# Re-ordering the start-up of a fused cosine-attention and feed-forward kernel: loads of batch 0, engine assignment, w_out's third quarter, and unit order

## The chip, the cores and the metric

The kernel runs on one core of a Trainium2 chip. The metric is device time in microseconds (us) of the whole program. Engines: PE (TensorE) multiplies matrices into PSUM; DVE (VectorE), ACT (ScalarE) and POOL (GpSimd) work element by element; SP (SyncE) issues nearly all DMAs. Each engine works through its own instructions in program order.

## The reference

Linear attention with cosine weights, then a feed-forward layer (batch 8, 8 heads, 576 positions, head size 64; w_in 512x2048, w_out 2048x512; all float32):

```python
theta = pi/2 * pos / 576
phi(x, c, s) = concat(relu(x)*c, relu(x)*s)        # 64 -> 128 features
q_p, k_p = phi(q, cos, sin), phi(k, cos, sin)
kv  = einsum('bhsf,bhsd->bhfd', k_p, v);  z = k_p.sum(over s)
num = q_p @ kv;  den = q_p @ z + 1e-6
x   = (num / den) -> (4608 tokens, 512)
h   = x @ w_in;  g = max(0.01*h, h);  out = g @ w_out
```

## The kernel before

Each batch has 512 main positions (four tiles j = 0..3 of 128) and 64 tail positions. Batch b's main positions form token group g = b; the tails of all batches are the ninth group. Everything is cast to float16 for PE.

For a group PE does this. `q_transpose` turns q_p of a tile (eight transposes), and an engine copies the result to `qpT`. `kv_half(b, hg)` multiplies k_p with v for heads 0-3 (hg 0) or 4-7 (hg 1), two extra columns of ones giving z; ACT copies the result to `kv`. `num_half(g, jp, hg)` multiplies qpT of two tiles (jp 0 or 1) with kv, and `divide` on DVE (three instructions) writes `xp`. `x_transpose_half` turns xp (four transposes) and ACT copies it to `xT`. The "half" forms serve groups 0 and 1; later groups use `kv_all`, `num`, `x_transpose`.

`ffn1(g, m)` is h for columns of w_in numbered m (16 of them): four products over the chunks c of 128 rows of w_in, 128x512 each, two m's to a PSUM tile, which ACT turns into `g` with one leaky relu. `ffn2(g, 4*tt + part)` is a unit of four products of w_out, with one quarter (`part`) of its rows, for output tile tt of the group; after part 3 `ffn2_out` copies the output tile to SBUF and stores it. `idle(n)` issues n products whose result nobody reads.

Loads go out from SP in program order: in the kernel before, q of batch 0 in two halves of heads, the tails of k and v (four pieces of 64 KB, rows of 256 bytes), k and v by halves of heads (`load_halves`), w_in in eight pieces of 512 KB, then two quarters of w_out, q of batch 1, its k and v tails, the other two quarters, k and v of batch 1 by halves, and so on. Loads share seven `stage` buffers. POOL casts w_in, DVE casts w_out.

The order of work is written out by hand up to the middle of group 1. From there `weave(units, steps)` runs through feed-forward units that have positions, and ahead of each unit emits every step (`at(pos, ...)`) whose position has come: q_p, k_p, kv, num and transposes of the next group. PSUM is three pools: `h` and `o` with two slots each, `n` with one.

Lines the steps touch: L417 is ffn1's product, L440 ffn2's, L260 and L270 the kv products, L374 and L391 the num_half products and the transposes, L220 and L222 phi on ACT and DVE, L291 and L395 ACT's kv and xT copies, L228 and L230 other copies and casts, L425 the leaky relu.

Of the kernel before, what the change touches and what calls it, by code (L numbers as in the profile page):

```python
# [9 lines left out]
dt = mybir.dt  # L10
# [3 lines left out]
P = 128  # L14
# [4 lines left out]
def kernel(  # L19
# [102 lines left out]
    w1 = [  # L122
        [const.tile([P, 2, 512], dt.float16, name=f"w1_{i}_{cp}") for cp in range(2)]
        for i in range(DFF // 512)
    ]
# [4 lines left out]

    w2v = moe_w_out.rearrange("(i p r) d -> i p r d", p=P, r=4)

    def load_w1(i, cp):

        if cp == 0:
            st["w1", i] = stage.tile([P, NKC, 512], dt.float32, name="w1st", tag="stage")
        sl = slice(2 * cp, 2 * cp + 2)
# [162 lines left out]
    def q_prep(g, j, lo=0, hi=H):  # L300
# [4 lines left out]
        phi_half(DVE, qp[:, lo:hi, 0:D], src[:, lo:hi], cos_t[:, c : c + 1])  # L305
        phi_half(DVE, qp[:, lo:hi, D:F], src[:, lo:hi], sin_t[:, c : c + 1])

    def q_transpose_dma(g, j):
        qpT = qptpool.tile([P, H, P], dt.float16, name="qpT")
# [53 lines left out]
            op=ALU.mult,  # L363
        )

    def num_half(g, jp, hg, where):

        if hg == 0:
            st["xp", g, jp] = qppool.tile([P, 2, H, D], dt.float16, name="xp", tag="qp")
        ps = psum(where, [P, 2, 512], dt.float32, "ps_numh")  # L370
        for o in range(2):
            for hh in range(4):
                h = 4 * hg + hh
                nc.tensor.matmul(  # L374
                    ps[:, o, hh * NE : (hh + 1) * NE],
                    lhsT=st["qpT", g, 2 * jp + o][:, h, :],
                    rhs=kv[g][:, h, :],
                )
        divide(ps, st["xp", g, jp][:, :, 4 * hg : 4 * hg + 4, :])

    def x_transpose_half(g, jp, hg, ps=None, out=True):
# [4 lines left out]
        if ps is None:  # L386
            ps = psum("o", [P, 2, 2 * P], dt.float16, "ps_xth")
        for cc in range(2):
            for o in range(2):
                h = 4 * hg + 2 * cc  # L390
                nc.tensor.transpose(  # L391
                    ps[:, cc, o * P : (o + 1) * P], xp[:, o, h : h + 2, :], ident
                )
        if out:
            nc.scalar.copy(  # L395
                st["xT", g][:, 2 * hg : 2 * hg + 2, jp * 2 * P : (jp + 1) * 2 * P], ps
            )

    def x_transpose(g, j, where="o"):
        xs = st["xs", g, j]  # L400
# [7 lines left out]
    def ffn1(g, m, lo=0, hi=MAIN, chunks=range(NKC), where="h"):  # L408

        if ("g", g) not in st:  # L410
            st["g", g] = gpool.tile([P, NFT, MAIN], dt.float16, name="g")
        if m % 2 == 0 and chunks[0] == 0 and lo == 0:
            st["h", m // 2] = psum(where, [P, 2, MAIN], dt.float32, "ps_h")
        xT = st["xT", g]
        ps = st["h", m // 2]
        for c in chunks:
            nc.tensor.matmul(  # L417
                ps[:, m % 2, lo:hi],
                lhsT=w1[m // 4][c // 2][:, c % 2, m % 4 : 512 : 4],
                rhs=xT[:, c, lo:hi],  # L420
                start=(c == 0 and lo == 0),
                stop=(c == NKC - 1 and hi == MAIN),
            )
        if m % 2 == 1 and chunks[-1] == NKC - 1 and hi == MAIN:
            nc.scalar.activation(st["g", g][:, m - 1 : m + 1, :], ps, AF.Lrelu)  # L425
# [59 lines left out]
    def cast_w1(i, cp, eng):  # L485
        sl = slice(2 * cp, 2 * cp + 2)
        copy(eng, w1[i][cp], st["w1", i][:, sl])

    def cast_w2(i, eng):
        copy(eng, w2[:, 4 * i : 4 * i + 4, :], st["w2", i])  # L490

    for hg in range(2):
        for j in range(2):
            q_prep(0, j, 4 * hg, 4 * hg + 4)
    for j in range(J):
        if j > 1:
            q_prep(0, j)
        q_transpose(0, j, ACT)  # L500
        idle(1)
    kp_tiles(0)
    k_tail(0, DVE, DVE)
    v_tail(0, DVE)
    for j in range(J):
        k_main(0, j, DVE, DVE, 0, 4)
    v_main(0, 0, 4, ACT)
    for j in range(2):
        k_main(0, j, ACT, DVE, 4, 8)
    idle(6)  # L510
    kv_half(0, 0, "o")
    for j in range(2, J):
        k_main(0, j, DVE, DVE, 4, 8)
    v_main(0, 4, 6, DVE)
    v_main(0, 6, 8, ACT)
    idle(1)
    num_half(0, 0, 0, "n")
    num_half(0, 1, 0, "h")
    idle(3)
    kv_half(0, 1, "o")  # L520
    for i in range(NB):
        for cp in range(2):
            cast_w1(i, cp, POOL)
    x_transpose_half(0, 0, 0)
    num_half(0, 0, 1, "n")
    half = 2 * P
    for m in range(2):
        ffn1(0, m, 0, half, range(0, 2))
    x_transpose_half(0, 1, 0)
    for m in range(2, 4):  # L530
        ffn1(0, m, 0, half, range(0, 2))
    num_half(0, 1, 1, "n")
    x_transpose_half(0, 0, 1)
# [37 lines left out]
    def at(pos, f, *args):  # L571
        steps.append((pos, lambda: f(*args)))
# [15 lines left out]
    cast_w2(3, DVE)  # L588
    ps = psum("n", [P, 2, DM], dt.float32, "ps_o")
    for tt in range(2):  # L590
        st["ps_o", 0, 2 + tt] = ps[:, tt]
    steps = []
    for j in range(J):
        at(5 + j, q_transpose, 1, j, ACT, "h")
        at(9, k_main, 1, j, ACT, DVE, 0, 4)
    at(9, v_main, 1, 0, 2, DVE)
    at(9, v_main, 1, 2, 4, ACT)
    order = [(0, 0), (1, 0), (2, 0), (3, 0), (0, 1), (1, 1), (2, 1), (3, 1), (2, 2), (3, 2)]
    weave([(n, f2(0, 4 * tt + part)) for n, (tt, part) in enumerate(order)], steps)
    for tt in (2, 3):  # L600
# [14 lines left out]
    ffn2(0, 3, None)  # L615
    kv_half(1, 1, "h")
    ffn2_out(0, 0, ACT)
    ffn2_mm(0, 1, 12, 14)
    num_half(1, 0, 1, "h")
    num_half(1, 1, 1, "h")  # L620
    ps = psum("n", [P, 2, MAIN], dt.float16, "ps_x")
    for jp in range(2):
        x_transpose_half(1, jp, 0, ps[:, :, jp * 2 * P : (jp + 1) * 2 * P], False)
    nc.scalar.copy(st["xT", 1][:, 0:2, :], ps)  # L624
    ffn2_mm(0, 1, 14, 16)
    ffn2_out(0, 1, DVE)
    ps = psum("o", [P, 2, 2, 2 * P], dt.float16, "ps_x1")
    x_transpose_half(1, 0, 1, ps[:, 0])
    for m in range(2):
        ffn1(1, m, 0, MAIN, range(0, 2))  # L630
    x_transpose_half(1, 1, 1, ps[:, 1])
    for m in range(2, 4):
        ffn1(1, m, 0, MAIN, range(0, 2))
    for m in range(4):
        ffn1(1, m, 0, MAIN, range(2, 4))

    units = []
    for m in range(4, NFT):  # L640
        units.append((8 + m / 2, f1(1, m, "n" if m < 6 else "h")))
    for g in range(1, NG):
        ahead = {1: 8, 2: 4}.get(g, 0)
        order = [f2(g, i) for i in range(ahead)]
# [33 lines left out]
            at(start + j * step + lag, q_transpose_dma, b, j)  # L678

    q_steps(2, 8, 0.4, 0.3)  # L680
    kv_steps(2, 9.7, 0.5, 13, DVE, 2)
    for j in range(J):
        at(13.5 + 1.1 * j, num, 2, j)
        at(14.8 + 1.1 * j, x_transpose, 2, j, "o" if j < 2 else "h")

    load_steps(3, 11, 13, 10)
    q_steps(3, 18, 0.8, 0.8)
# [50 lines left out]
```

## Time and profile before

| | |
|---|---|
| median of 3 runs | 295.70 us (295.67 to 295.79) |
| the profiled execution | 296.48 us, its span 294.7 us |
| granted TensorE clock | 1.00 |
| PE busy | 286.4 us, 97% |
| DVE, ACT, POOL busy | 129.9, 117.9, 11.0 us |
| DMA | 56.93 MB, 193 GB/s on average |

The span runs from the first to the last instruction; what lies around it (1.8 us here) is in the time as well. In a timeline row the first number is the start from the span's beginning, the second the duration of one instruction (or from the first to the last end of several), then engine, line, operation, output and inputs, and in brackets the idle time before it and what ended it. Products on PE overlap: one of 128x512 is followed by the next 0.216 us later, though each is shown longer.

### The profile page before, as it was taken

The numbers are of one execution on the slowest core, as the hardware profiler recorded it, in microseconds if no ns is written. First come the engines' busy times: TensorE is split into PE (matmuls) and PEld (weight loads), VectorE is DVE, ScalarE is ACT, GpSimd is POOL, SyncE is SP. The second block draws the span as 40 slices with busy tenths as digits, with TensorE's granted clock in tenths as the row PEclk, the third lists the DMA queues.
The fourth block names the chain that finished last, engine by engine and source line by source line (L and its number), as shares of the span: only waits on it lengthen the run. The fifth ranks groups of instructions, "written<-read, shape, count | busy, mean of one in ns | idle before, by whom it ended". The sixth has DMA issues, their size and how long they took to land.

```text
span 294.7 us, 4802 instructions
## 1 busy us (share of the span) xinstructions
PE 286.4 (97%) x1932; PEld 153.9 (52%) x1932; DVE 129.9 (44%) x329; ACT 117.9 (40%) x143; POOL 11.0 (4%) x20
## 2 busy tenths in 40 slices
PE   7799999999999999999999999999999999999995
PEld 3585556565465455555545554555445544444444
DVE  6951488945846816823562356233323211000011
ACT  4846366754352722642263226322222232222200
POOL 2064000000000000000000000000000000000000
PEclk9999999999999999999999999999999999999999
DMA  7999999999999999989683997416671211011132
GB/s 222 361 385 406 325 362 331 300 155 336 232 271 325 179 265 335 178 158 332 171 152 82 292 276 148 107 55 145 145 160 51 73 53 38 36 46 60 39 71 71
DMA packets 88773, 56.93 MB, mean 193 GB/s; under 512 B 56880, under 2 KB 81712, under 8 KB 88240
## 3 DMA queue, kind: packets, MB, share of 16 engines
q1 hardware_dynamic: 88672, 56.57, 74.2%
q8 instruction: 15, 0.25, 0.4%
q14 instruction: 6, 0.05, 0.1%
q10 hardware_dynamic: 80, 0.07, 0.1%
HBM read 36.70 MB, written 9.44 MB: 157 GB/s over the span
## 4 chain that ended last, share of the span: by engine, by line
PE 81%; DMA 8%; SPq 6%; ACT 1%; issue 1%; DVE 1%; ACTq 0%
PE ps_h L417 38%; PE ps_o L440 37%; SPq L96 4%; DMA w2st<-in_moe_w_out_dram 4%; DMA w1st<-in_moe_w_in_dram 4%; PE ps_num L339 3%; PE ps_kv L270 2%; SPq L86 1%; DMA out_dram<-osb 1%; SPq L138 1%; ACT vmain L228 1%; SPq L142 1%; PE ps_kv L260 1%; DVE w L230 0%; PE ps_numh L374 0%
## 5 line engine op out<-in xcount | busy, mean ns | idle before, releaser
L417 PE MATMUL ps_h<-xT,w 128*128 128x512 f16 (+1 forms) x592 | 142.6, 373 | 0.3 <-ACT xT L624 0.2
L440 PE MATMUL ps_o<-w,g 128*128 128x512 f16 x560 | 139.5, 379 | 0.3 <-DVE w L230 0.3
L425 ACT ACTIVATE g<-ps_h 128x1024 f16<-128x1024 f32 x72 | 73.5, 1024 | 132.9 <-PE ps_h L417 132.7
L417 PEld LDWEIGHTS <-w 128*128 128x128 f16 x592 | 64.4, 113 | 52.3 <-issue 0.3
L440 PEld LDWEIGHTS <-g 128*128 128x128 f16 x560 | 54.1, 98 | 62.0 <-issue 0.6
L230 DVE COPY osb<-ps_o 128x512 f32<-128x512 f32 x34 | 23.4, 690 | 80.1 <-PE ps_o L440 80.1
L350 DVE TENSOR_SCALAR den<-ps_num 128x8 f32<-128x8 f32 x28 | 4.6, 166 | 52.9 <-PE ps_num L339 52.9
L355 DVE TENSOR_TENSOR xs<-ps_num,rden 128x512 f16<-128x512 f32 x28 | 19.4, 691 | 1.0
L222 DVE TENSOR_SCALAR qp<-qst,cos_t 128x512 f16<-128x512 f32 (+1 forms) x34 | 15.8, 465 | 4.9 <-DMA qst<-in_q_dram 4.9
L222 DVE TENSOR_SCALAR kpm<-kst,sin_t 128x512 f16<-128x512 f32 (+1 forms) x40 | 16.5, 428 | 0.8 <-DMA kst<-in_k_dram 0.8
L222 DVE TENSOR_SCALAR qp<-qst,sin_t 128x512 f16<-128x512 f32 (+1 forms) x34 | 15.8, 465 | 0.0
L339 PEld LDWEIGHTS <-qpT 128*128 128x128 f16 (+1 forms) x256 | 11.2, 101 | 7.3 <-issue 1.7
L222 DVE TENSOR_SCALAR kpm<-kst,cos_t 128x512 f16<-128x512 f32 (+1 forms) x29 | 13.0, 449 | 0.1
L228 ACT CAST vmain<-vst 128x1024 f16<-128x1024 f32 (+1 forms) x14 | 12.9, 953 | 0.4 <-DMA vst<-in_v_dram 0.3
L339 PE MATMUL ps_num<-kv,qpT 128*128 128x66 f16 (+1 forms) x256 | 12.4, 194 | 0.0
L270 PEld LDWEIGHTS <-kpm 128*128 128x128 f16 x256 | 10.5, 97 | 2.6 <-DVE kpm L222 0.7
L228 ACT COPY qpT<-ps_qt 128x1024 f16<-128x1024 f16 x8 | 7.8, 1019 | 7.0 <-PE ps_qt L329 7.0
L162 PE MATMUL ps_idle<-blank 128*128 128x512 f16 x28 | 9.1, 462 | 1.2 <-DVE blank L157 1.2
L230 DVE CAST w<-w2st 128x2048 f16<-128x2048 f32 x4 | 4.9, 1228 | 10.7 <-DMA w2st<-in_moe_w_out_dram 10.7
L230 POOL CAST w<-w1st 128x1024 f16<-128x1024 f32 x8 | 8.3, 1042 | 15.1 <-DMA w1st<-in_moe_w_in_dram 15.0
L270 PE MATMUL ps_kv<-vmain,kpm 128*128 128x66 f16 x192 | 8.1, 193 | 0.0
L354 DVE RECIPROCAL rden<-den 128x8 f32<-128x8 f32 x36 | 7.3, 203 | 1.2
(57 smaller groups left out, 97.1 us busy)
## 6 DMA issues: line engine op xcount, KB each, us to landing
out_dram<-osb SPq DMA_DIRECT2D x32, 256.0 KB, 2.5
qst<-in_q_dram SPq DMA_DIRECT2D x7, 1024.0 KB, 6.5
kst<-in_k_dram SPq DMA_DIRECT2D x6, 1024.0 KB, 8.8
vst<-in_v_dram SPq DMA_DIRECT2D x6, 1024.0 KB, 8.9
w1st<-in_moe_w_in_dram SPq DMA_DIRECT2D x8, 512.0 KB, 11.0
w2st<-in_moe_w_out_dram SPq DMA_DIRECT2D x4, 1024.0 KB, 11.5
kst<-in_k_dram SPq DMA_DIRECT2D x4, 512.0 KB, 8.7
vst<-in_v_dram SPq DMA_DIRECT2D x4, 512.0 KB, 8.7
```

The lines of the kernel that those rows point to most:

```text
L96: nc.sync.dma_start(t[o * TAIL : (o + 1) * TAIL], v4[o])
L162: nc.tensor.matmul(ps, lhsT=blank[:, 0:P], rhs=blank)
L222: eng.tensor_scalar(out=o, in0=i, scalar1=0.0, scalar2=col, op0=ALU.max, op1=ALU.mult)
L228: nc.scalar.copy(o, i)
L230: eng.tensor_copy(o, i)
L270: nc.tensor.matmul(ps[:, (2 * cc + o) * NE : (2 * cc + o + 1) * NE], lhsT=kpm[:, h, j, :], rhs=vmain[b % 2][:, h, j, :], start=False, stop ...
L339: nc.tensor.matmul(ps[lo:hi, h // 4, (h % 4) * NE : (h % 4 + 1) * NE], lhsT=qpT[:, h, lo:hi], rhs=kv[b][:, h, :],)
L354: nc.vector.reciprocal(rden, den)
L355: nc.vector.tensor_tensor(out=xs, in0=ps[:, :, 0 : 4 * NE].rearrange("p a (b e) -> p a b e", e=NE)[:, :, :, 0:D], in1=rden.rearrange("p (a ...
L417: nc.tensor.matmul(ps[:, m % 2, lo:hi], lhsT=w1[m // 4][c // 2][:, c % 2, m % 4 : 512 : 4], rhs=xT[:, c, lo:hi], start=(c == 0 and lo == 0 ...
L425: nc.scalar.activation(st["g", g][:, m - 1 : m + 1, :], ps, AF.Lrelu)
L440: nc.tensor.matmul(st["ps_o", g, tt], lhsT=st["g", g][:, m, tt * P : (tt + 1) * P], rhs=w2[:, m, :], start=(m == 0), stop=(m == NFT - 1),)
```

## The change

Loads of batch 0: k's tails go ahead of k's first half and v's tails behind it. w_in's first piece of two chunks is loaded and cast as two pieces of one. w_out's third quarter is loaded ahead of batch 1's k and v tails. Engines: ACT does q_p of tile 3 and all second-half cosines of batch 0, POOL casts v's tails and a part of v, DVE copies the fourth qpT; in group 1 ACT copies all of output tiles (0,0) and (0,1). In group 0's w_out the order is by quarter over all four output tiles, and the last two quarters are cast by halves. Batch 1's num halves, transposes and the first ffn1 products stand in another order, with the xT copies by halves, and batch 2's kv and num steps one position later.

```diff
+    w1 = {}            # tiles of 2 chunks, but w1[0,0] and w1[0,1] of 1 each
...
     load_kvtail("k", k, 0)
+    load_main("k", k, 0, (0,))
     load_kvtail("v", v, 0)
-    load_halves(0)
-    for i in range(NB):
-        for cp in range(2):
-            load_w1(i, cp)
+    load_main("v", v, 0, (0,))
+    load_main("k", k, 0, (1,))
+    load_main("v", v, 0, (1,))
+    w1_parts = [(0, 0, 1), (0, 1, 1), (0, 2, 2)]
+    for i in range(1, NB):
+        w1_parts += [(i, 0, 2), (i, 2, 2)]
+    for part in w1_parts:
+        load_w1(*part)
...
     for hg in range(2):
-        for j in range(2):
-            q_prep(0, j, 4 * hg, 4 * hg + 4)
+        for j in range(J):
+            q_prep(0, j, 4 * hg, 4 * hg + 4, ACT if j == 3 else DVE)
+    kp_tiles(0)
+    q_transpose(0, 0, ACT)
+    idle(1)
+    q_transpose(0, 1, ACT)
+    idle(1)
+    k_tail(0, DVE, DVE)
+    v_tail(0, POOL)
+    k_main(0, 0, ACT, DVE, 0, 4)
+    for j in range(1, J):
+        k_main(0, j, DVE, DVE, 0, 4)
+    v_main(0, 0, 2, DVE)
+    v_main(0, 2, 4, ACT)
+    q_transpose(0, 2, ACT, "n")
+    idle(1)
+    q_transpose(0, 3, DVE)
+    idle(7)
+    kv_half(0, 0, "o")
     for j in range(J):
-        ... (the order before: L497-L540)
+        k_main(0, j, ACT, DVE, 4, 8)
+    num_half(0, 0, 0, "h")
+    num_half(0, 1, 0, "n")
+    v_main(0, 4, 6, ACT)
+    v_main(0, 6, 8, POOL)
     idle(6)
+    x_transpose_half(0, 0, 0)
     kv_half(0, 1, "o")
+    for part in w1_parts:
+        cast_w1(*part, POOL)
+    x_transpose_half(0, 1, 0)
     half = 2 * P
+    ps = psum("h", [P, 2, 512], dt.float32, "ps_numh")
     for m in range(2):
-        ffn1(0, m, 0, half, range(0, 2))
+        ffn1(0, m, 0, half, range(0, 1))
+    num_half(0, 0, 1, None, ps)
+    num_half(0, 1, 1, "n")
+    for m in range(2):
+        ffn1(0, m, 0, half, range(1, 2))
+    for m in range(2):
+        ffn1(0, m, half, MAIN, range(0, 2))
+    x_transpose_half(0, 0, 1)
     for m in range(2, 4):
         ffn1(0, m, 0, half, range(0, 2))
-    for m in range(4):
+    for m in range(2, 4):
         ffn1(0, m, half, MAIN, range(0, 2))
     x_transpose_half(0, 1, 1)
...
     load_main("q", q, 1)
+    load_w2(2)
     load_kvtail("k", k, 1)
     load_kvtail("v", v, 1)
-    for i in range(2, 4):
-        load_w2(i)
+    load_w2(3)
...
-    cast_w2(2, DVE)
+    cast_w2(2, DVE, 0, 2)
+    cast_w2(2, DVE, 2, 4)      # cast_w2(3) alike
...
-        at(5 + j, q_transpose, 1, j, ACT, "h")
+        at(6 + j, q_transpose, 1, j, ACT, "h")
-    order = [(0, 0), (1, 0), (2, 0), (3, 0), (0, 1), (1, 1), (2, 1), (3, 1), (2, 2), (3, 2)]
+    order = [(tt, part) for part in range(3) for tt in range(J)]
...
     ffn2_out(0, 2, DVE)
     ffn2_out(0, 3, DVE)
-    ffn2(0, 2)
+    ffn2(0, 3, None)
+    ffn2_out(0, 0, ACT)
     kv_half(1, 0, "h", False)
     k_main(1, 0, ACT, DVE, 4, 8)
     kv_half_out(1, 0)
...
-    ffn2(0, 4 + 2)
+    ffn2_mm(0, 1, 12, 14)
     num_half(1, 0, 0, "h")
     num_half(1, 1, 0, "n")
-    ... (the order before: L615-L635)
+    ffn2_mm(0, 1, 14, 16)
+    x_transpose_half(1, 0, 0)
+    ffn2_out(0, 1, ACT)
     kv_half(1, 1, "h")
+    x_transpose_half(1, 1, 0)
     num_half(1, 0, 1, "h")
+    num_half(1, 1, 1, "n")
     for m in range(2):
         ffn1(1, m, 0, MAIN, range(0, 2))
+    x_transpose_half(1, 0, 1)
     for m in range(2, 4):
         ffn1(1, m, 0, MAIN, range(0, 2))
+    x_transpose_half(1, 1, 1)
+    for m in range(4, 6):
+        ffn1(1, m, 0, MAIN, range(0, 2), "n")
+    for m in range(6):
+        ffn1(1, m, 0, MAIN, range(2, 4))
...
-    kv_steps(2, 9.7, 0.5, 13, DVE, 2)
+    kv_steps(2, 9.7, 0.5, 14, DVE, 2)      # num and x_transpose of batch 2: + 1 as well
```

More of the change, by code (lines that the diff above doesn't have):

```diff
@@ L119, in load_halves @@
             load_main("v", v, b, (hg,))
[L122 to L125, printed above, removed]
+    w1 = {}
+    for i in range(DFF // 512):
+        for c in range(0, NKC, 2):
+            n = 1 if i == 0 and c == 0 else 2
+            for cc in range(c, c + 2, n):
+                t = const.tile([P, n, 512], dt.float16, name=f"w1_{i}_{cc}")
+                for d in range(n):
+                    w1[i, cc + d] = (t, d)
     w2 = const.tile([P, NFT, DM], dt.float16, name="w2")
@@ L131, with load_w1 @@
     w2v = moe_w_out.rearrange("(i p r) d -> i p r d", p=P, r=4)
-    def load_w1(i, cp):
-        if cp == 0:
+    def load_w1(i, c, n):
+        if c == 0:
             st["w1", i] = stage.tile([P, NKC, 512], dt.float32, name="w1st", tag="stage")
-        sl = slice(2 * cp, 2 * cp + 2)
+        sl = slice(c, c + n)
         nc.sync.dma_start(st["w1", i][:, sl], w1v[:, sl, 512 * i : 512 * (i + 1)])
@@ L298, in q_src, with q_prep @@
         return st["qt", j], J, [(2 * j, 0, TAIL), (2 * j + 1, TAIL, P)]
-    def q_prep(g, j, lo=0, hi=H):
+    def q_prep(g, j, lo=0, hi=H, eng=DVE):
         src, c, _ = q_src(g, j)
@@ L304, in q_prep @@
         qp = st["qp", g, j]
-        phi_half(DVE, qp[:, lo:hi, 0:D], src[:, lo:hi], cos_t[:, c : c + 1])
-        phi_half(DVE, qp[:, lo:hi, D:F], src[:, lo:hi], sin_t[:, c : c + 1])
+        phi_half(eng, qp[:, lo:hi, 0:D], src[:, lo:hi], cos_t[:, c : c + 1])
+        phi_half(eng, qp[:, lo:hi, D:F], src[:, lo:hi], sin_t[:, c : c + 1])
     def q_transpose_dma(g, j):
@@ L364, in divide, with num_half @@
         )
-    def num_half(g, jp, hg, where):
+    def num_half(g, jp, hg, where, ps=None):
         if hg == 0:
             st["xp", g, jp] = qppool.tile([P, 2, H, D], dt.float16, name="xp", tag="qp")
-        ps = psum(where, [P, 2, 512], dt.float32, "ps_numh")
+        if ps is None:
+            ps = psum(where, [P, 2, 512], dt.float32, "ps_numh")
         for o in range(2):
@@ L379, in num_half, with x_transpose_half @@
         divide(ps, st["xp", g, jp][:, :, 4 * hg : 4 * hg + 4, :])
-    def x_transpose_half(g, jp, hg, ps=None, out=True):
+    def x_transpose_half(g, jp, hg, out=True):
         if ("xT", g) not in st:
@@ L385, in x_transpose_half @@
         xp = st["xp", g, jp]
-        if ps is None:
-            ps = psum("o", [P, 2, 2 * P], dt.float16, "ps_xth")
+        ps = psum("o", [P, 2, 2 * P], dt.float16, "ps_xth")
         for cc in range(2):
@@ L393, in x_transpose_half, with x_transpose_half_out @@
                 )
+        st["xth", g, jp, hg] = ps
         if out:
-            nc.scalar.copy(
-                st["xT", g][:, 2 * hg : 2 * hg + 2, jp * 2 * P : (jp + 1) * 2 * P], ps
-            )
+            x_transpose_half_out(g, jp, hg)
+    def x_transpose_half_out(g, jp, hg):
+        nc.scalar.copy(
+            st["xT", g][:, 2 * hg : 2 * hg + 2, jp * 2 * P : (jp + 1) * 2 * P],
+            st["xth", g, jp, hg],
+        )
     def x_transpose(g, j, where="o"):
@@ L418, in ffn1 @@
                 ps[:, m % 2, lo:hi],
-                lhsT=w1[m // 4][c // 2][:, c % 2, m % 4 : 512 : 4],
+                lhsT=w1[m // 4, c][0][:, w1[m // 4, c][1], m % 4 : 512 : 4],
                 rhs=xT[:, c, lo:hi],
@@ L483, in last_tile @@
             queue.dma_start(out[r0 : r0 + TAIL, cols], osb[o * TAIL : (o + 1) * TAIL, :])
[L485 to L490, printed above, removed]
-    for hg in range(2):
-        for j in range(2):
-            q_prep(0, j, 4 * hg, 4 * hg + 4)
-    for j in range(J):
[L498 to L508, printed above, removed]
+    def cast_w1(i, c, n, eng):
+        copy(eng, w1[i, c][0], st["w1", i][:, c : c + n])
+    def cast_w2(i, eng, lo=0, hi=4):
+        copy(eng, w2[:, 4 * i + lo : 4 * i + hi, :], st["w2", i][:, lo:hi])
+    for hg in range(2):
+        for j in range(J):
+            q_prep(0, j, 4 * hg, 4 * hg + 4, ACT if j == 3 else DVE)
@@ L510 @@
+    v_main(0, 4, 6, ACT)
+    v_main(0, 6, 8, POOL)
     idle(6)
[L511 to L519, printed above, removed]
-    kv_half(0, 1, "o")
[L521 to L525, printed above, removed]
+    x_transpose_half(0, 0, 0)
+    kv_half(0, 1, "o")
@@ L526 @@
+    for part in w1_parts:
+        cast_w1(*part, POOL)
+    x_transpose_half(0, 1, 0)
     half = 2 * P
+    ps = psum("h", [P, 2, 512], dt.float32, "ps_numh")
     for m in range(2):
-        ffn1(0, m, 0, half, range(0, 2))
-    x_transpose_half(0, 1, 0)
+        ffn1(0, m, 0, half, range(0, 1))
[6 more added lines that the diff above has]
+    x_transpose_half(0, 0, 1)
@@ L530 @@
     for m in range(2, 4):
         ffn1(0, m, 0, half, range(0, 2))
-    num_half(0, 1, 1, "n")
-    x_transpose_half(0, 0, 1)
-    for m in range(4):
+    for m in range(2, 4):
         ffn1(0, m, half, MAIN, range(0, 2))
@@ L587 @@
     v_tail(1, DVE)
-    cast_w2(3, DVE)
+    cast_w2(3, DVE, 0, 2)
+    cast_w2(3, DVE, 2, 4)
     ps = psum("n", [P, 2, DM], dt.float32, "ps_o")
@@ L593 @@
     for j in range(J):
-        at(5 + j, q_transpose, 1, j, ACT, "h")
-        at(9, k_main, 1, j, ACT, DVE, 0, 4)
-    at(9, v_main, 1, 0, 2, DVE)
-    at(9, v_main, 1, 2, 4, ACT)
-    order = [(0, 0), (1, 0), (2, 0), (3, 0), (0, 1), (1, 1), (2, 1), (3, 1), (2, 2), (3, 2)]
+        at(6 + j, q_transpose, 1, j, ACT, "h")
+    order = [(tt, part) for part in range(3) for tt in range(J)]
     weave([(n, f2(0, 4 * tt + part)) for n, (tt, part) in enumerate(order)], steps)
+    for j in range(J):
+        k_main(1, j, ACT, DVE, 0, 4)
+    v_main(1, 0, 2, DVE)
+    v_main(1, 2, 4, ACT)
     for tt in (2, 3):
@@ L611 @@
     v_main(1, 6, 8, ACT)
-    ffn2(0, 4 + 2)
+    ffn2_mm(0, 1, 12, 14)
     num_half(1, 0, 0, "h")
     num_half(1, 1, 0, "n")
-    ffn2(0, 3, None)
+    ffn2_mm(0, 1, 14, 16)
+    x_transpose_half(1, 0, 0)
+    ffn2_out(0, 1, ACT)
     kv_half(1, 1, "h")
-    ffn2_out(0, 0, ACT)
-    ffn2_mm(0, 1, 12, 14)
+    x_transpose_half(1, 1, 0)
     num_half(1, 0, 1, "h")
[L620 to L628, printed above, removed]
+    num_half(1, 1, 1, "n")
     for m in range(2):
         ffn1(1, m, 0, MAIN, range(0, 2))
-    x_transpose_half(1, 1, 1, ps[:, 1])
+    x_transpose_half(1, 0, 1)
     for m in range(2, 4):
         ffn1(1, m, 0, MAIN, range(0, 2))
-    for m in range(4):
+    x_transpose_half(1, 1, 1)
+    for m in range(4, 6):
+        ffn1(1, m, 0, MAIN, range(0, 2), "n")
+    for m in range(6):
         ffn1(1, m, 0, MAIN, range(2, 4))
     units = []
-    for m in range(4, NFT):
-        units.append((8 + m / 2, f1(1, m, "n" if m < 6 else "h")))
+    for m in range(6, NFT):
+        units.append((8 + m / 2, f1(1, m)))
     for g in range(1, NG):
@@ L680 @@
     q_steps(2, 8, 0.4, 0.3)
-    kv_steps(2, 9.7, 0.5, 13, DVE, 2)
+    kv_steps(2, 9.7, 0.5, 14, DVE, 2)
     for j in range(J):
-        at(13.5 + 1.1 * j, num, 2, j)
-        at(14.8 + 1.1 * j, x_transpose, 2, j, "o" if j < 2 else "h")
+        at(14.5 + 1.1 * j, num, 2, j)
+        at(15.8 + 1.1 * j, x_transpose, 2, j, "o" if j < 2 else "h")
     load_steps(3, 11, 13, 10)
```

## Prediction

> **What bounds the kernel now.** I read the page first, its busy table and its slices.
>
> ```profile
> PE 286.4 (97%) x1932; PEld 153.9 (52%) x1932; DVE 129.9 (44%) x329; ACT 117.9 (40%) x143; POOL 11.0 (4%) x20
> PE   7799999999999999999999999999999999999995
> DMA  7999999999999999989683997416671211011132
> ```
>
> PE is full but for the first slices, so only the start-up can give anything. The stage table (busy time by window) says where: PE is busy 16.32 of the first 20 us (padding included), all of 20 to 42, 10.36 of the 11 us from 42 to 53, then 49.00 of 49.00. What the first 53 us win or lose therefore reaches the end unchanged. The rows of the timeline show three places.
>
> ```profile
> 12.65 0.61 DVE L222 TENSOR_SCALAR kpm<-kst,sin_t 128x256 f16<-128x256 f32 x2 [0.50 <-DMA kst<-in_k_dram]
> ...
> 19.87 12.27 PE L417 MATMUL ps_h<-xT,w 128*128 128x256 f16 x64
> ```
>
> *Start.* DVE waits for the second half of k until 12.65; PE then limps until the last transposes of batch 0, and runs without a hole from 19.87.
>
> ```profile
> 40.67 1.89 PE L440 MATMUL ps_o<-w,g 128*128 128x512 f16 x8
> 41.62 1.23 DVE L230 CAST w<-w2st 128x2048 f16<-128x2048 f32 x1 [0.34 <-DMA w2st<-in_moe_w_out_dram]
> 42.90 2.75 PE L440 MATMUL ps_o<-w,g 128*128 128x512 f16 x12 [0.34 <-DVE w L230]
> 45.48 0.22 PE L260 MATMUL ps_kvh<-vtail,kpt 128*128 128x132 f16 x1
> ```
>
> *w_out.* One 128x512 product costs 0.216 us (0.864 for a unit of four). The eight at 40.67 are issued by 42.40; the next start at 42.90, when the last quarter is cast: 0.50 lost.
>
> ```profile
> 49.26 0.38 ACT L291 CAST kv<-ps_kvh 128x264 f16<-128x264 f32 x1 [1.01 <-PE ps_kvh L270]
> 49.54 0.59 ACT L228 COPY osb<-ps_o 128x512 f32<-128x512 f32 x1
> 49.69 0.67 PE L374 MATMUL ps_numh<-kv,qpT 128*128 128x66 f16 x16
> 50.85 1.01 ACT L624 COPY xT<-ps_x 128x1024 f16<-128x1024 f16 x1 [0.72 <-PE ps_x L391]
> 51.91 1.02 PE L417 MATMUL ps_h<-xT,w 128*128 128x512 f16 x4 [0.18 <-ACT xT L624]
> 52.99 7.29 PE L417 MATMUL ps_h<-xT,w 128*128 128x512 f16 x33
> ```
>
> *Batch 1.* From 45.48 (its first kv product) to 52.99 PE follows the chain kv copy, division, transposes, xT copy. Here ACT copies kv before it empties the output tile of 49.54, and spare w_out units fill most of the chain: about 0.8 is idle (0.20, 0.25 and 0.36 are its largest holes).
>
> Durations used below, from these and neighbouring rows (step from one to the next of a kind, and latency): DVE 128x256 0.265; ACT relu 128x256 0.41; ACT copy of 128x512 0.52 (0.59); kv copy 0.37; a division 0.20 + 0.24 + 0.61, xp ready 1.17 after its start; kv half on PE 0.63, a num_half 0.25, four transposes 0.22; from a last product to its reader 0.21, from a copy to PE 0.05.
>
> **The change part by part.**
>
> *Loads of batch 0.* The bytes ahead of k's second half are the same, so I leave it at 12.65 (v's at 14.14); only k's first half comes earlier. By the time of the issues (DMA part of the page, narrowed to windows) the four tail pieces landed between 6.16 and 7.3, 1.15 us for 0.26 MB; half of that moves behind k's first half (8.87, now 8.3), which is not what is waited for.
>
> *Start, engines.* DVE now does four sines from 12.65, free at 13.71 (the cosines go to ACT: 12.65 + 4 x 0.41 = 14.29, v heads 4 and 5 cast by 14.95). First division from 13.71, xp at 14.88, transposes, kv half 15.10 to 15.73, kv copy to 16.36, num_half 16.39 and 16.64. Third division 16.86, its transposes at 18.03, eight half products (0.86), last transposes 19.11 to 19.34. Before, 19.87: **-0.5**. Filled holes: the copy of the fourth qpT goes to DVE (a PSUM row of 512 took 0.69, twice that 1.4; either way done by 12.1, ahead of 12.65, else it pushes the sines one for one). v's tail casts on POOL cost between 0.29 (DVE's row of that size) and 0.62 (POOL's 128x512) each; landed at 8.95 they end by 10.2, while PE is padded until 10.8. Both cost 0.
>
> *w_in's first load in two.* The first piece is half as long, castable at 14.85 and 0.62 later done; PE reads it at 16.2, so cover is 0.7 and the gain 0. One more issue on SP: 0.4 to 0.7, hidden under a full queue (w_in loads land 11 us after issue). The trace's 512 KB pieces came every 1.35 us, the 1 MB pieces of w_out every 2.6, some 4% more bytes per us. The Trainium skill (DMA: Bandwidth & Descriptors, Rules for kernel authors) wants 1 MiB or more per DMA for full bandwidth, which speaks against this split; a further 4% of 0.7 us would be an estimated 0.03 more by it, and 0 by the queue's rows.
>
> *Third quarter of w_out ahead of batch 1's tails; unit order by part.* PE starts w_out at 31.98 - 0.5 = 31.48. The third quarter is now wanted after eight units and three transposes of q (0.45 each): 31.48 + 6.91 + 1.35 = 39.74. DVE reaches its cast when q of batch 1 (landed 34.96, eight operations of 0.395) is done, 38.12; a half cast is 1.23/2, about 0.65: ready 38.8, cover 0.9, if the load is there by then. It landed at 39.0 behind the tails, which took 1.6 (34.96 to 36.6); ahead of them about 37.4. Left where it was, its first half would be ready at 39.7, also just in time. The last quarter (41.6, first half ready 42.3) is wanted only after twelve units: 31.48 + 10.37 + 1.8 = 43.65. The 0.50 goes: **-0.5**. PE is next late nowhere until 15 units are done, at 46.24, where before it had done 13 at 45.48: ahead by 2 x 0.864 - 0.76 = 0.97.
>
> *Batch 1's order.* From 46.2, two of the fill units are used up, and ACT empties output tile (0,0) before the cosine and the kv copy: the tile's last product ends at 46.2, so ACT copies it from 46.40 to 46.92, the cosine ends 47.33, kv is ready at 47.75. PE has finished kv half and two w_out products at 47.25: idle **0.50**. num_halves to 48.26, two products to 48.69; the division starts 48.22, xp 49.39: idle **0.70**. Transposes, kv half to 50.24; the second xp at 50.46: **0.23**. ACT now has xT (to 50.33), output tile (0,1) (50.85), and only then kv, 51.27, with PE free at 50.69: **0.59**. Then 0.06 for xT and 0.21 for the third division. Last transposes end at 54.21. Idle 2.3 where it was 0.8: **+1.45**. The loads do not set this: v's last half lands at 47.65, its cast ends 49.1, wanted at 49.7.
>
> *Batch 2 a unit pair later.* DVE no longer copies tile (0,1) but ends its divisions at 53.8; k and v of batch 2 are ready at 61.7, wanted at 63.0 (twelve units in), so one position later covers it. ACT, with three activations (0.92 each) and two cosines of 0.63 in a row, frees the ps_h of units 6 and 7 at 61.24, PE wants it at 61.12: **+0.1**. The last xT copy (0.21 + 0.59 + 0.05 = 0.85) stands behind one unit, 0.864: 0.
>
> Sum: -0.5 - 0.5 + 1.45 + 0.1 = **+0.55**. The profiled execution took 296.48 (span 294.7 and 1.8 around it), so 297.05 for one like it; the median is 295.70, 0.78 below, so **296.3**.
>
> **The rivals.**
>
> *Loads come earlier (faster).* k's second half landed 2.35 after v's first, where its neighbours are 1.43 to 1.57 apart, and the tails moved 0.26 MB in 1.15 where 512 KB pieces would have taken 0.73. If breaking up the tails removes both, k's second half lands 0.8 + 0.45 earlier, near 11.4, and the whole start with it (w_in's and v's pieces too): 296.3 - 1.25 = 295.0. It decides from about 11.5, beyond which the start gains over 1.1 more. For it: q of batch 1, with tails queued behind it, also took 4.6 where a later q took 3.0. Against it: the number of small pieces is unchanged. The Trainium skill (DMA: Bandwidth & Descriptors, Specifications) puts the line rate at transfers of 512 B or more, with read-modify-write below, and tail rows are 256 B; by that rule the tails cost the same wherever they stand, and the start stays at -0.5, as the unchanged 1.15 would have it. No row shows tails apart, so 0.16.
>
> *Third quarter late (slower still).* If it lands after 39.1, every tenth adds: an issue here waits for the load eight places ahead (v's first half of batch 1 issues at 35.00, when q landed at 34.96), which orders the queue anew. At 39.5 it costs 0.5: 296.8. Chance 0.12.
>
> *The start gains nothing.* If one of ACT's longer tasks in 12.65 to 16.4 runs 0.5 late, 296.8; ACT's queue is full there. Chance 0.08.
>
> *The move does nothing, and batch 1's chain costs less.* DVE is held by q to 38.12 in any case, so the third quarter's place is worth nothing by the sum already; if ACT's copies overlap PE so that only 0.7 of the 1.45 appears, -0.5 - 0.5 + 0.8 = -0.2: 295.5. Chance 0.10.
>
> **How the numbers follow.** Forecast 0.54, with 0.3 either way from twelve waits of 0.05 to 0.25 each: 295.9 to 296.7. A difference of 0.2% (0.59 us) is about what a measurement of this kernel can tell from no change; the line lies at 296.29, in the middle of the forecast. Slower: half of 0.54 and 0.12 and 0.08, with a little for mishaps, 0.49. Same: the other half and 0.10, less that little, 0.35. Faster: 0.16. The range takes in the fast rival and a slow one with both extras: 295.0 to 297.1.
>
> **What would show it.** The 64-product row of w_in starting at 19.3 to 19.4, not 19.87; DVE's sines still waiting for k until 12.6; no wait of PE for a cast of w_out; the first kv product of batch 1 near 46.2; then waits of PE for the kv copy (twice, 0.5 each) and for xp (0.7), and the last transposes of batch 1 ending near 54.2. The prediction is wrong if k's second half lands before 12, if PE waits for w_out near 39.7, or if the idle time between 46 and 54 is under 1.5.

## The result and the profile after

The changed kernel takes 296.75 us (median; 296.56 to 296.92), the kernel before beside it 295.69 (295.48 to 295.91). The ratio is 1.0036, with a 95% interval of 1.0023 to 1.0049: slower by 1.06 us. The forecast was 296.3 in a range of 295.0 to 297.1; direction and range held, the size was 0.6 for 1.06. The profiled execution took 296.56 (span 294.8).

The page of the changed kernel, its busy table and PE's slices:

```profile
PE 286.9 (97%) x1934; PEld 153.8 (52%) x1934; DVE 128.8 (44%) x326; ACT 119.8 (41%) x151; POOL 12.7 (4%) x24
PE   8999997999999999999999999999999999999995
```

The first slices are fuller than before, but the seventh (44 to 52 us) has come down to 7: that is batch 1.

Its timeline, start:

```profile
11.87 1.14 DVE L231 TENSOR_SCALAR kpm<-kst,sin_t 128x256 f16<-128x256 f32 x4 [0.32 <-DMA kst<-in_k_dram]
18.58 12.61 PE L431 MATMUL ps_h<-xT,w 128*128 128x256 f16 x64
18.60 1.04 POOL L239 CAST w<-w1st 128x1024 f16<-128x1024 f32 x1 [1.48 <-DMA w1st<-in_moe_w_in_dram]
19.97 1.04 POOL L239 CAST w<-w1st 128x1024 f16<-128x1024 f32 x1 [0.33 <-DMA w1st<-in_moe_w_in_dram]
21.07 9.65 PEld L431 LDWEIGHTS <-w 128*128 128x128 f16 x46 [0.62 <-POOL w L239]
31.03 2.32 PE L454 MATMUL ps_o<-w,g 128*128 128x512 f16 x10
```

The block of 64 products starts at 18.58, much earlier than forecast, and then PE's weight loads wait 0.62 for the piece of w_in that POOL casts from 19.97. That piece came right behind one that landed late (POOL waited 1.48 for that one). w_out's first product is at 31.03.

Its timeline, w_out and batch 1 (PE and DVE, then ACT):

```profile
40.58 5.34 PE L454 MATMUL ps_o<-w,g 128*128 128x512 f16 x24
45.10 1.29 DVE L239 COPY osb<-ps_o 128x512 f32<-128x512 f32 x2 [1.10 <-PE ps_o L454]
45.76 0.22 PE L269 MATMUL ps_kvh<-vtail,kpt 128*128 128x132 f16 x1
47.27 0.67 PE L384 MATMUL ps_numh<-kv,qpT 128*128 128x66 f16 x16 [0.30 <-ACT kv L300]
48.40 0.69 DVE L364 TENSOR_TENSOR xp<-ps_numh,rden 128x512 f16<-128x512 f32 x1
49.15 0.40 PE L400 MATMUL ps_xth<-ident,xp 128*128 128x128 f16 x4 [0.77 <-DVE xp L364]
50.99 0.67 PE L384 MATMUL ps_numh<-kv,qpT 128*128 128x66 f16 x16 [0.39 <-ACT kv L300]
53.73 0.39 PE L400 MATMUL ps_xth<-ident,xp 128*128 128x128 f16 x4
```

```profile
45.96 0.59 ACT L237 COPY osb<-ps_o 128x512 f32<-128x512 f32 x1 [1.67 <-PE ps_o L454]
46.85 0.37 ACT L300 CAST kv<-ps_kvh 128x264 f16<-128x264 f32 x1
50.06 0.59 ACT L237 COPY osb<-ps_o 128x512 f32<-128x512 f32 x1
50.54 0.40 ACT L300 CAST kv<-ps_kvh 128x264 f16<-128x264 f32 x1
```

PE does 24 products of w_out without waiting for a cast, then has little left to do between the steps of batch 1. Twice ACT empties an output tile ahead of the kv copy for which PE waits, and the first xp comes late because DVE empties two output tiles before the operations of k.

To weigh the runs I use a ledger of three numbers, all from PE's rows. (1) w_out's first product. (2) The wait between it and batch 1's first kv product, beyond 0.864 a unit and 0.45 for each of the four q transposes. (3) PE's unfilled time from that kv product to the end of the last transposes: the interval less 0.63 for a kv half, 0.25 for a num_half, 0.22 for four transposes and 0.216 for each 128x512 product in it. In the changed kernel the interval is 45.76 to 53.95, 8.19 us, with 5.73 of work (two kv halves, four num halves, four times four transposes, 12 products): 2.46. The last three columns compare the ledger's sum, the span (given to 0.1) and the profiled time with the repeat of the kernel before.

| profiled execution | (1) | (2) | (3) | sum, against the repeat | span, against 293.6 | time, against 295.43 |
|---|---|---|---|---|---|---|
| before, first profile | 31.98 | 0.47 | 0.91 | +1.02 | +1.1 | +1.05 |
| before, repeated | 31.53 | 0 | 0.81 | 0 | 0 | 0 |
| start only | 31.08 | 0.69 | 0.91 | +0.34 | +0.3 | +0.63 |
| rest only | 31.48 | 0 | 2.43 | +1.57 | +1.7 | +1.60 |
| changed kernel | 31.03 | 0 | 2.46 | +1.15 | +1.2 | +1.13 |
| copies behind kv (ACT) | 31.05 | 0 | 2.34 | +1.05 | +1.1 | +1.02 |
| third quarter behind tails | 31.01 | 0 | 2.46 | +1.13 | +1.2 | +1.11 |
| first loads as before | 31.06 | 0 | 2.46 | +1.18 | +1.2 | +1.15 |
| unit held | 30.86 | 0 | 1.35 | -0.13 | -0.1 | -0.11 |
| chain reordered | 31.18 | 0 | 0.36 | -0.80 | -0.8 | -0.68 |
| chain reordered, repeated | 31.02 | 0 | 0.36 | -0.96 | -0.9 | -0.84 |
| chain, old start | 31.50 | 0 | 0.37 | -0.47 | -0.4 | -0.43 |
| copies back (DVE) | 30.97 | 0 | 0.69 | -0.68 | -0.7 | -0.39 |
| copies back, repeated | 30.97 | 0 | 0.69 | -0.68 | -0.7 | -0.37 |

The sum agrees with the span within 0.15 us in every row, and with the time too, but for start only and the two rows with the copies back, whose times are 0.3 above. That 0.3 lies outside the span, where no row can show it: time less span is 2.05 to 2.16 in every execution of these kernels, 1.88 to 1.96 in those of the reordered chain, and 1.73 to 1.87 in all others. What makes it stays open.

### The profile page after: what moved, and what is told of

Same layout as the page of the kernel before. It is cut to its first block, busy times and chain, and to the rows that moved or that the text cites. A ratio compares the mean times of both kernels' runs of the same rounds, so it can differ in the third digit from the quotient of the medians.

```text
span 294.8 us, 4818 instructions
## 1 busy us (share of the span) xinstructions
PE 286.9 (97%) x1934; PEld 153.8 (52%) x1934; DVE 128.8 (44%) x326; ACT 119.8 (41%) x151; POOL 12.7 (4%) x24
## 4 chain that ended last, share of the span: by engine, by line
PE 87%; DMA 4%; SPq 3%; DVE 2%; ACT 2%; issue 1%; POOL 0%; ACTq 0%
PE ps_h L431 41%; PE ps_o L454 39%; DMA w1st<-in_moe_w_in_dram 4%; PE ps_num L348 3%; PE ps_kv L279 2%; SPq L86 1%; SPq L96 1%; SPq L142 1%; DMA out_dram<-osb 1%; DVE osb L239 1%; ACT vmain L237 1%; PE ps_qt L338 1%; DVE kpm L231 1%; PE ps_kv L269 1%; DVE xp L364 0%
## 5 line engine op out<-in xcount | busy, mean ns | idle before, releaser
L239 DVE COPY osb<-ps_o 128x512 f32<-128x512 f32 x33 | 22.7, 691 | 81.0 <-PE ps_o L454 81.0
L364 DVE TENSOR_TENSOR xs<-ps_num,rden 128x512 f16<-128x512 f32 x28 | 19.4, 691 | 1.0
L231 DVE TENSOR_SCALAR kpm<-kst,cos_t 128x512 f16<-128x512 f32 (+1 forms) x26 | 12.1, 466 | 0.0
L171 PE MATMUL ps_idle<-blank 128*128 128x512 f16 x30 | 10.0, 480 | 1.2 <-DVE blank L166 1.2
L239 DVE CAST w<-w2st 128x1024 f16<-128x1024 f32 (+1 forms) x6 | 5.0, 868 | 12.8 <-DMA w2st<-in_moe_w_out_dram 12.7
L237 ACT COPY qpT<-ps_qt 128x1024 f16<-128x1024 f16 x7 | 7.0, 1012 | 5.8 <-PE ps_qt L338 5.8
L239 POOL CAST w<-w1st 128x1024 f16<-128x1024 f32 (+1 forms) x9 | 8.5, 945 | 3.9 <-DMA w1st<-in_moe_w_in_dram 3.8
```

What stands on the lines that cost most here:

```text
L171: nc.tensor.matmul(ps, lhsT=blank[:, 0:P], rhs=blank)
L231: eng.tensor_scalar(out=o, in0=i, scalar1=0.0, scalar2=col, op0=ALU.max, op1=ALU.mult)
L237: nc.scalar.copy(o, i)
L239: eng.tensor_copy(o, i)
L364: nc.vector.tensor_tensor(out=xs, in0=ps[:, :, 0 : 4 * NE].rearrange("p a (b e) -> p a b e", e=NE)[:, :, :, 0:D], in1=rden.rearrange("p (a ...
```

## The experiments

**The kernel before again.** No edit.

> The kernel before, unchanged, profiled once more. Theory A: the profiled execution of before (296.48, 0.78 above its median) was an unusual one, in which the loads were late: k's second half at 12.65, the last quarter of w_out at 41.6. A new profile then shows k's second half near 11.9, the last quarter near 40.6, PE waiting for it no more than 0.1, and a span near 293.9. Rival B: the rows were typical and the 0.78 lies outside the span or later in it: the new profile shows 12.6 and 41.6 again, and PE losing 0.5 before its first product of the last quarter.

Measured: 295.43 in the profiled execution, 295.77 the median beside it. PE and DVE rows of this repeat's timeline:

```profile
19.42 12.27 PE L417 MATMUL ps_h<-xT,w 128*128 128x256 f16 x64
31.53 0.81 PE L440 MATMUL ps_o<-w,g 128*128 128x512 f16 x3
40.22 4.48 PE L440 MATMUL ps_o<-w,g 128*128 128x512 f16 x20
40.57 1.23 DVE L230 CAST w<-w2st 128x2048 f16<-128x2048 f32 x1 [0.37 <-DMA w2st<-in_moe_w_out_dram]
```

POOL's row for the piece of w_in that the changed kernel waits for:

```profile
19.93 1.04 POOL L230 CAST w<-w1st 128x1024 f16<-128x1024 f32 x1 [1.43 <-DMA w1st<-in_moe_w_in_dram]
```

The 20 products run on where the first profile had a hole of 0.50: the last quarter is cast from 40.57 instead of 41.62, as all loads of that stretch come about 1.0 earlier. The wait for w_out belonged to the execution that was profiled, not to every run of the kernel. The median lies 0.34 above this repeat; how much of the wait a median run has, no trace shows.

**Batch 0's part alone.** The loads of batch 0, w_in's pieces and the division of batch 0's work as changed; from the loads of w_out on, all as before.

> Only the change of batch 0: its loads, w_in's first piece in two, its engines and its order; w_out's loads, the unit order, batch 1 and batch 2 as before. Theory A (the start gains, batch 1's order loses 1.45): w_out's first product near 31.0 as in the changed kernel, part of that given back where w_out's last quarter or v of batch 1 is waited for, 0.2 to 0.5 below the kernel before: 295.2 to 295.5. Rival C (the new start itself is the loss, PE waits for w_in that arrives no earlier): 296.2 or above.

Measured: 295.78, ratio 1.0004 (0.9993 to 1.0014): no gain, a miss. PE's timeline of this run:

```profile
39.78 1.89 PE L455 MATMUL ps_o<-w,g 128*128 128x512 f16 x8
42.22 2.75 PE L455 MATMUL ps_o<-w,g 128*128 128x512 f16 x12 [0.55 <-DVE w L239]
```

w_out starts 0.45 earlier, and the old unit order then reaches the last quarter before it is there: the wait of the first profile again. In this execution the cast (from 40.94) also comes 0.37 later than in the repeat, which had about 0.15 to spare, so the wait eats more than the start gains. The medians tell it otherwise: the median span is 0.3 shorter than that of the kernel before (293.7 for 294.0), inside the gain that was expected, and the 0.3 more outside the span takes it back.

**The rest alone.** Batch 0 as before, all behind it as changed.

> The rest of the change without batch 0's part: third quarter of w_out ahead, unit order by quarter, casts by halves, batch 1's order, batch 2's steps one later. Theory A: nothing is gained by w_out's move in a run whose loads are on time, so the whole of batch 1's 1.45 and the 0.1 show: 297.1 to 297.4. Rival C: the loss lies in the start, so this is at 295.7 or below.

Measured: 297.34, ratio 1.0053 (1.0039 to 1.0067), +1.57 and as expected. PE waits 0.29 for kv, 0.74 for xp and 0.39 for kv: the changed kernel's waits, 0.45 later.

**ACT's output copies behind the kv copies.**

```diff
-    ffn2_out(0, 0, ACT)
     kv_half(1, 0, "h", False)
     k_main(1, 0, ACT, DVE, 4, 8)
     kv_half_out(1, 0)
+    ffn2_out(0, 0, ACT)
...
-    ffn2_out(0, 1, ACT)
     kv_half(1, 1, "h")
+    ffn2_out(0, 1, ACT)
```

> The changed kernel, with ACT emptying output tiles (0,0) and (0,1) after it has copied kv, not before. Theory A (PE's two waits for kv, 0.30 and 0.39 in the changed kernel's rows, are ACT's order): those two rows lose most of their wait, the wait for xp stays at 0.5 to 0.8, 296.75 - 0.4 to 0.5 = 296.3. Rival D (the chain is set by the divisions alone, so the time moves into the wait for xp): 296.7.

Measured: 296.58, ratio 1.0028 (1.0019 to 1.0037): 0.17 below the changed kernel, by intervals that overlap; the ledger has 0.12 less in batch 1. PE's timeline of this run:

```profile
47.04 0.67 PE L384 MATMUL ps_numh<-kv,qpT 128*128 128x66 f16 x16
49.22 0.40 PE L400 MATMUL ps_xth<-ident,xp 128*128 128x128 f16 x4 [1.08 <-DVE xp L364]
```

The first wait for kv is gone, and the wait for xp has grown from 0.77 to 1.08: DVE is busy with two output copies and five operations of k until 48.04 in any case. With so few products left, removing one wait lengthens the next.

**One unit held back as fill.**

```diff
     order = [(tt, part) for part in range(3) for tt in range(J)]
+    order.remove((1, 2))
...
     v_main(1, 6, 8, ACT)
-    ffn2_mm(0, 1, 12, 14)
+    ffn2(0, 4 + 2)
     num_half(1, 0, 0, "h")
     num_half(1, 1, 0, "n")
-    ffn2_mm(0, 1, 14, 16)
+    ffn2_mm(0, 1, 12, 16)
```

> The changed kernel with one unit of four products moved: (1,2), tile 1 with w_out's third quarter, leaves the row by quarters and stands between batch 1's first kv half and the first half divisions, where the kernel before has it. Theory A (the order by quarters spends ahead of batch 1's chain the products that hid it): everything ahead of the first kv product comes 0.86 us earlier (four products at 0.216), the last quarter of w_out, cast by 41.8, is still not waited for (its first product would be at 42.3), the wait for the kv copy of 0.30 at 47.27 in the changed kernel goes, and that for xp at 49.15 gets no longer: last transposes near 53.0 instead of 53.73, 296.0 us, -0.7 against the changed kernel. Rival B (VectorE sets the first division, whatever TensorE has to do): the wait for xp grows by what the others lose, 296.5 to 296.7.

Measured: 295.68, ratio 0.9999 (0.9991 to 1.0008): 1.07 less than the changed kernel, more than the 0.7 expected. PE's timeline of this run:

```profile
46.25 0.67 PE L384 MATMUL ps_numh<-kv,qpT 128*128 128x66 f16 x16
47.89 0.40 PE L400 MATMUL ps_xth<-ident,xp 128*128 128x128 f16 x4
49.73 0.67 PE L384 MATMUL ps_numh<-kv,qpT 128*128 128x66 f16 x16 [0.39 <-ACT kv L300]
```

Four products (0.86 us) now stand between the first kv half and the num halves and four between these and the transposes. The first wait for kv has gone, PE's unfilled time before the first xp has fallen from 0.94 to 0.27, and the second wait for kv is still 0.39; w_out is still not waited for. All work, engines and copies are the changed kernel's, so holding back four products gives 1.1 of the 1.65 that the ledger shows lost in batch 1 (2.46 for 0.81).

**Batch 1's chain in another order.**

```diff
     order = [(tt, part) for part in range(3) for tt in range(J)]
+    order.remove((1, 2))
...
     for tt in (2, 3):
         ffn2(0, 4 * tt + 3, None)
-    ffn2_out(0, 2, DVE)
-    ffn2_out(0, 3, DVE)
-    ffn2(0, 3, None)
-    ffn2_out(0, 0, ACT)
-    kv_half(1, 0, "h", False)
+    kv_half(1, 0, "h")
     k_main(1, 0, ACT, DVE, 4, 8)
-    kv_half_out(1, 0)
+    ffn2(0, 3, None)
     for j in range(1, J):
-        k_main(1, j, ACT if j < 3 else DVE, DVE, 4, 8)
+        k_main(1, j, ACT, DVE, 4, 8)
     v_main(1, 4, 6, POOL)
-    v_main(1, 6, 8, ACT)
-    ffn2_mm(0, 1, 12, 14)
+    v_main(1, 6, 8, POOL)
     num_half(1, 0, 0, "h")
-    num_half(1, 1, 0, "n")
-    ffn2_mm(0, 1, 14, 16)
+    ffn2_out(0, 0, ACT)
+    num_half(1, 1, 0, "h")
+    ffn2(0, 4 + 2)               # held back, as above
+    ffn2_mm(0, 1, 12, 14)
+    ffn2_out(0, 3, ACT)
     x_transpose_half(1, 0, 0)
-    ffn2_out(0, 1, ACT)          # now on DVE, ahead of the last transposes
     kv_half(1, 1, "h")
+    ffn2_mm(0, 1, 14, 16)
+    ffn2_out(0, 2, DVE)
     x_transpose_half(1, 1, 0)
```

> The changed kernel with the unit (1,2) held back as before and batch 1's chain in another order: the first kv half right behind the units (2,3) and (3,3), its copy first on ScalarE, all eight second-half operations of k ahead of VectorE's output copies, units (0,3), (1,2) and (1,3) as fill, tile 3's output copy on ScalarE, tile 2's behind the second kv half, v's second half on GpSimd alone. Theory A: batch 1's idle time is a matter of order alone; TensorE's waits of 1.5 us there shrink to under 0.6, the last transposes end near 52.3 and, with the start that the change gains, 295.2 us, below both kernels (-1.5 and -0.5). Rival B (VectorE's work between the arrival of k's second half and the first division is the bound): its output copies leave that stretch here, so that even then some is gained, 295.9 to 296.3. Rival C: GpSimd's two casts of v (0.42 each in the rows, twice as many here) hold the second kv half, with a wait of TensorE for v near 48, 296.

Measured: 294.75, ratio 0.9969 (0.9958 to 0.9981): below both kernels, 2.0 under the changed one. Its timeline, rows of ACT, DVE and PE:

```profile
45.02 0.38 ACT L300 CAST kv<-ps_kvh 128x264 f16<-128x264 f32 x1 [0.61 <-PE ps_kvh L279]
45.21 1.14 DVE L231 TENSOR_SCALAR kpm<-kst,sin_t 128x256 f16<-128x256 f32 x4 [1.08 <-DMA kst<-in_k_dram]
45.68 0.67 PE L384 MATMUL ps_numh<-kv,qpT 128*128 128x66 f16 x16
47.52 0.38 PE L400 MATMUL ps_xth<-ident,xp 128*128 128x128 f16 x4
```

ACT copies kv as soon as it is there, DVE works on k as soon as its second half lands, and PE's unfilled time falls to 0.36. The last transposes start at 51.80. No wait for v was seen, so GpSimd's casts cost nothing, though the two took 1.17 (the 0.42 of the expectation is GpSimd's row for 64x256, and these are 128x512).

**w_out's third quarter behind the tails again.**

```diff
-    load_w2(2)
     load_kvtail("k", k, 1)
     load_kvtail("v", v, 1)
+    load_w2(2)
```

> The changed kernel with the load of w_out's third quarter behind batch 1's tails again, as in the kernel before. The prediction held this move to be worth nothing: the third quarter's cast is then about 0.9 us later (near 37.6 instead of 36.66), its first product comes at 38.0 or later, and the tails' operations have until the kv products at 45.7. Expected: no wait of TensorE for w_out's third quarter and 296.75, within 0.15 of the changed kernel. Rival: the tails' issue on SyncE holds the quarter longer and TensorE waits for it, 0.2 to 0.6 us more.

Measured: 296.79, 0.04 from the changed kernel, as expected. In this run's timeline DVE casts the quarter 1.36 later than in the changed kernel (36.66), and PE goes on:

```profile
38.02 1.29 DVE L239 CAST w<-w2st 128x1024 f16<-128x1024 f32 x2 [0.76 <-DMA w2st<-in_moe_w_out_dram]
40.57 5.34 PE L454 MATMUL ps_o<-w,g 128*128 128x512 f16 x24
```

**First loads as before.**

```diff
-    load_main("k", k, 0, (0,))
     load_kvtail("v", v, 0)
+    load_main("k", k, 0, (0,))
     load_main("v", v, 0, (0,))
```

> The changed kernel with the first batch's loads in the order of before (v's tails ahead of k's first half), the division of work and all else kept. If the start's gain of 0.45 us comes from the load order, k's first half comes 0.5 us later, w_out's first product near 31.45 instead of 31.03, and the time is 297.1 to 297.2. If it comes from the division of the work among the engines, 296.75, no difference.

Measured: 296.91 (296.58 to 296.94), 0.16 from the changed kernel and within the spread of both. PE's rows of its timeline:

```profile
18.96 12.27 PE L431 MATMUL ps_h<-xT,w 128*128 128x256 f16 x64
21.09 9.66 PEld L431 LDWEIGHTS <-w 128*128 128x128 f16 x46 [0.27 <-POOL w L239]
```

The block starts 0.38 later than in the changed kernel, waits 0.35 less for w_in, and w_out's first product is at 31.06 (31.03 there). So in these executions the place of v's tails gains nothing that lasts, as w_in's piece (cast from 19.99 here) sets when w_out starts; whether it would gain if w_in came earlier stays open. The start's 0.45 comes from the division of the work; the split of w_in's first load was not run apart.

**The reordered chain with the old start.** Batch 0 and its loads as in the kernel before, the rest as in the reordered chain.

> Batch 0 and its loads as in the kernel before, all behind it as in the run with the reordered chain (the unit (1,2) held back, k's second half ahead of VectorE's output copies). Theory A (the start's gain of 0.45 us adds to whatever batch 1's order gains, as long as nothing waits for w_out): 295.2, 0.45 above the reordered chain and 0.5 below the kernel before. Rival: with the start 0.45 later the chain meets the same arrivals with more slack and hides the difference, 294.8 to 295.0.

Measured: 295.20, ratio 0.9986 (0.9977 to 0.9995), 0.45 above the reordered chain (0.6 by the median spans, 293.4 for 292.8): the start's gain, whole, now that no wait for w_out stands behind it.

**DVE's output copies put back ahead of k.** From the reordered chain:

```diff
+    ffn2_out(0, 2, DVE)
+    ffn2_out(0, 3, DVE)
     kv_half(1, 0, "h")
...
-    ffn2_out(0, 3, ACT)
...
-    ffn2_out(0, 2, DVE)
```

> The run with the reordered chain, with one thing put back: both output copies of tiles 2 and 3 on VectorE, ahead of k's second-half operations. If VectorE's copies there set the first division, the operations of k start at about 45.7 instead of 45.21, xp comes 0.5 later, its wait is seen in TensorE's row near 47.5 (0.3 to 0.5), and the time is 295.1 to 295.3. If the copies fit into VectorE's idle time before k's second half lands (1.08 us there at 45.21), nothing changes: 294.75 to 294.85, and the gain of the reordered chain over the held unit is that of the other moves (the kv half first, its copy first on ScalarE).

Measured: 295.31, ratio 0.9992 (0.9983 to 1.0001). DVE's rows of its timeline:

```profile
44.18 1.29 DVE L239 COPY osb<-ps_o 128x512 f32<-128x512 f32 x2
45.38 1.13 DVE L231 TENSOR_SCALAR kpm<-kst,sin_t 128x256 f16<-128x256 f32 x4
```

The operations of k start 0.17 later than without the copies, and the ledger finds 0.33 in batch 1, yet the medians differ by 0.56. So both were run side by side, unchanged:

> The run with the reordered chain again, unchanged, beside the one with the copies put back, so that the two are compared on one chip. Theory A (the copies ahead of k's operations cost): 294.8, 0.5 below the other. Rival (the 0.56 between their medians came of other loads or another chip, as the traces of the two, 0.1 us apart by batch 2, suggest): the medians lie within 0.2 of each other.

> The run with the copies put back again, unchanged, beside the reordered chain. Theory A: 295.3, and if this execution's trace is one of the longer ones, k's operations on VectorE stand behind the copies and TensorE waits for xp near 47.5. Rival: within 0.2 of the reordered chain's median.

Measured: 294.76 (ratio 0.9964, 0.9952 to 0.9977) and 295.25 (0.9985, 0.9976 to 0.9995). The 0.5 is real, but the traces do not lay it to the copies. PE's rows of the first profile with the copies back:

```profile
44.22 0.41 PE L279 MATMUL ps_kvh<-vmain,kpm 128*128 128x66 f16 x8
47.61 0.40 PE L400 MATMUL ps_xth<-ident,xp 128*128 128x128 f16 x4
```

The kv products of 44.22 come 0.18 later than PE could start them (0.26 in the repeat). They start as DVE's cast of v, begun at 43.73, ends, and DVE's output copies stand behind that cast. Only 0.16 (0.07 in the repeat) of the ledger's 0.33 is a wait for xp, where the expectation had 0.3 to 0.5. Of the medians' 0.5, about 0.3 is in the spans (293.1 for 292.8) and 0.2 outside them (2.13 for 1.95); where the longer spans lose what the profiled ones do not, and what lies outside, stays open. With the copies back the ledger of batch 1 is still 0.66 below that of the held unit (0.69 for 1.35), so most of what the reordering adds comes from its other moves.

## Why the prediction was right in direction and short in size

*Start, -0.5: right by luck, as two errors cancel.* w_out's first product is 0.50 earlier than in the repeat (31.03 for 31.53), and alone this part moves it by 0.45. But the row of 64 products starts at 18.58, not 19.3 to 19.4, which is 0.84 ahead of the repeat's 19.42; 12.11 after its start, as in the repeat, w_out would have begun at 30.69. The other 0.34 went to a wait that the sum left out: the fourth 512 KB of w_in is cast from 19.93 in the repeat and from 19.97 here, so it comes no earlier for an earlier start. In all ten profiles with the new start that cast begins at 19.81 to 20.13, and w_out's first product follows 11.05 to 11.07 behind it. The division of the work gains 0.84, and w_in's load cuts it to 0.50.

k's second half landed by 11.87 and not at 12.65. Before 12 was a sign set for the prediction being wrong, and this part of it was: the sum took 12.65 from an execution with late loads. The earlier landing is no work of the change, as in the repeat of the kernel before ACT's second-half cosines start at 12.01 without a wait. Over all profiles but the first, k's second half landed at 11.9 to 12.2 in the four with v's tails ahead of k's first half, and at 11.9 to 12.1 in the nine with them behind it. The Trainium skill (DMA: Bandwidth & Descriptors, Specifications) puts the line rate at transfers of 512 B or more, and tail rows have 256 B wherever they stand; the landings agree that their place does not matter, but no run times the tails apart.

*w_out's last quarter, -0.5: the step that failed.* It was read from an execution 0.78 above its own median, and the ledger shows why that one was long: 0.45 at w_out's start, 0.47 in this wait and 0.10 in batch 1, in all 1.02 of its 1.05 above the repeat. The sum took the wait off as a gain, and then took the 0.78, which held it, off again on the way to the median. Against the repeat the term is 0. (The sum itself, 296.48 + 0.55, is 297.03 and not 297.05, which changes nothing.)

*Batch 1's order, +1.45: right, 0.2 small.* The waits forecast were 0.50, 0.70, 0.23, 0.59, 0.06 and 0.21, 2.29 in all; PE's steps in the profile after give 0.45, 0.94, 0.21, 0.55, 0 and 0.28, 2.43 (2.46 in the ledger). The kernel before has 0.81 (0.8 was used): +1.65, and +1.57 by the medians of the rest alone. Its cause was named as fill used up and ACT's order. The held unit shows that fill is most of it (2.46 to 1.35), and that ACT's order alone is worth 0.1 to 0.2, since DVE bounds the same stretch, which the prediction did not say.

*Third quarter's place, 0: right.* *Batch 2, +0.1: right in size.* From the end of the ledger to the first product of group 2's feed-forward the changed kernel loses 0.05 more than the repeat (76.17 for 74.97 is 1.20, of which the ledger has 1.15). It lies where it was forecast: ACT's third activation in a row there ends at 60.86, and PE's next product starts at 60.91, 0.05 late.

*w_in's first load in two, 0.* POOL cast both small pieces in one row of 1.28 from 14.07 without a pause, and the piece that PE later waits for is cast from 19.82 to 19.98 without the split too. The 0.03 estimated from the Trainium skill's rule on the size of a DMA (DMA: Bandwidth & Descriptors, Rules for kernel authors) is too little for any run here to show, and no run has the split alone.

Corrected: -0.50 + 0 + 1.65 + 0.05 = +1.20 by the traces, where the profiled times differ by 1.13 and the medians by 1.06.

## What to carry to other kernels

When a profiled execution lies above its median, a wait in it may be that distance: either take the wait off or the distance, not both, and profile the kernel before twice. A unit order that suits the arrival of weights may spend the independent work that hides a later chain of small steps; count how many units stand between those steps before and after. Where a chain crosses three engines, taking one wait away may be worth little (0.1 to 0.2 here) until the order on all of them is changed together. Compare spans beside times: kernels here differ by up to 0.3 in what lies outside the span, which no timeline shows.

## What the runs showed of the hardware

Loads land at other times from one execution to the next: in two profiles of the kernel before, k's second half landed at 12.65 and by 12.01, and w_out's last quarter was cast from 41.62 and from 40.57. One load is late in every profile, the fourth of w_in: behind its first cast of w_in POOL waits longest for that one, 0.70 in the first profile and 1.17 to 1.48 in the thirteen others, where the waits behind it are near 0.32; why, no run tells. A PSUM copy of 128x1024 from float16 to float16 took DVE 0.68, half of the 1.4 that the prediction bounded it by.
